# Turning attention rows by TensorE transposes of four blocks instead of a VectorE transpose and four transfers per block

## The chip, the cores and the metric

The kernel runs on one core of a Trainium2 chip. The metric is the device time of one launch in microseconds (us). Before the change it is 474.96 us, the median of 3 runs (473.96 to 475.51). A difference of 0.3% is about what a measurement of this kernel can tell.

## The reference

Two stages follow each other. The first is linear attention with a decay per head (4 batches, 8 heads, 768 positions, head size 64), computed in blocks: each block takes its own masked scores and a running state. The second is a mixture of experts (3072 tokens of 512 features, 8 experts, hidden size 1024, one expert per token).

```
for b in range(nb):                                   # blocks of 64 positions
    intra = (qb @ kb^T * Dmask) @ vb
    inter = (qb * lam_pow) @ kv_state
    out[:, :, sl] = intra + inter
    kv_state = lam_block * kv_state + (kb * rev_pow)^T @ vb
x = out as rows of 512 features, one per token
logits = x @ w_gate + modality_bias[modality_id]
e_idx = argmax(logits);  gate_w = softmax(logits)[e_idx]
for e in range(8):                                    # tokens of expert e
    out[mask] = gate_w[mask] * (relu(x[mask] @ w1[e]) @ w2[e])
```

All is in fp32; the kernel's experts use three products of split fp32 parts per product.

## The kernel before

**Attention.** There are 24 blocks g of 128 tokens (4 batches of 6). A loop over m = 0 to 11 (lines 819 to 888) works on a pair of blocks a = 2m and b = 2m+1. In step m it issues, in this order: `scores` and `mask` of the next pair, `keys` (ScalarE scales the keys, kd, 16 instructions for two blocks) and `query` (GpSimd), then `from_state` and `values` of this pair, whose result `o` in PSUM ScalarE copies to `xt` (line 283), then `products` of the next pair (they need kd), which give the state (`add`, VectorE). Every second step `gates` computes the router's logits of four blocks. Input pairs are fetched into four slots: `load(m + 4)`, 2 MB, is issued on ScalarE's queue in step m (line 88), after the copies of that step.

**The turn.** `o` holds features on partitions; rows to be scattered need tokens on partitions. `turn` (line 287) transposes 32x32 squares of one block on VectorE (`xt` to `xn`), and `spread` (line 301) moves `xn` with four transfers of 64 KB on SP's queue into `grp`, a buffer of 8 token tiles whose rows have 512 features and 16 words of tags. A token tile holds 32 tokens of each of four blocks. 96 such transfers are made.

**Routing.** For each of three groups of 8 token tiles, VectorE chooses experts and slots; GpSimd scatters each tile's rows to the buffer `placed` in HBM (`one_slot`, line 389), which is ordered by expert. `aside` (line 797) says in which step how many of them are issued. Lists of work (`listA`, `listB`, `listC`) are computed for the experts as soon as enough tokens are counted.

**Experts.** A tile of 256 tokens is fetched from `placed` (`fetch_x`, into `xg`), turned on VectorE (`turn_rows`, line 659), and goes through `first_layer` (w1) and `second` (w2); the result `y` is scattered to the output. Tiles 0 to 3 start while the routing still goes on; then come two thin tiles (64 and 32 tokens) and eight more wide ones. Weights are fetched by `fetch_w1` and `fetch_w2`, four transfers each, only if the expert differs from the one before. The scatter leaves the rows behind each expert's last token undefined; `clear_ends` (line 611) writes 256 blank rows there for each of 8 experts, ahead of the fetches of the thin tiles.

**What sets the order.** The orders of TensorE, VectorE, ScalarE and SP are those in which the code is written. Each transfer of SP's and ScalarE's queues signals one of eight counters in turn, and one that is to use a counter again waits until the transfer before it on that counter has landed. A transfer that waits holds up everything behind it on its engine.

Of the kernel before, what the change touches and what calls it, by code (L numbers as in the profile page):

```python
# [15 lines left out]
P = 128  # L16
# [16 lines left out]
RC = B * NC // RN  # L33
GR = B * NC // 4
MIN_WIDE = 8
MAX_WIDE = 17
# [6 lines left out]
def linear_attention_moe(tc, qkv, lam, modality, wg, mbias, w1, w2, out):  # L43
    nc = tc.nc
    with ExitStack() as ctx:
# [105 lines left out]
        def gpsimd_constants():  # L151
            pool(nc.gpsimd.memset(onesb, 1.0))
            pool(nc.gpsimd.affine_select(out=lowb, in_=onesb, pattern=[[1, P]], compare_op=ALU.is_gt,
                                         fill=0.0, base=0, channel_multiplier=-1))
            loose_iota = dict(channel_multiplier=0, allow_small_or_imprecise_dtypes=True)
            pool(nc.gpsimd.iota(desc, pattern=[[-1, E]], base=E, **loose_iota))
            pool(nc.gpsimd.memset(pay, 0))
            for t in range(4):
                mine = pay[t * Q : (t + 1) * Q].rearrange("q (g t) w -> q g t w", t=4)
                pool(nc.gpsimd.iota(mine[:, :, :, 0:1], pattern=[[4 * P, GR], [Q, 4]], base=t * P, channel_multiplier=1))  # L160
# [114 lines left out]
        def values(g):  # L275
            c = g % NC
            vt, op, pt = loaded(g)[2], ops.pop(g), pts.pop(g)
            for p in range(NP):
                for hl in range(2):
                    nc.tensor.matmul(op[place(g, hl), p, :], vt[:, (2 * p + hl) * D : (2 * p + hl + 1) * D],  # L280
                                     pt[:, hl, p, :], start=(c == 0 and p == 0), stop=(p == NP - 1))
            xts[g] = work.tile([P, NP, P], F32, name="xt", bufs=6)
            nc.scalar.copy(out=xts[g], in_=op)  # L283

        xns = {}
# [8 lines left out]
        def group(g):  # L294

            n = B * NC // RN
            if g % n == 0:
                groups.append(work.tile([P, 2 * 4 * RW], F32, name="grp", tag="grp", bufs=RN))
            return groups[g // n].rearrange("p (g c w) -> p g c w", g=2, c=4)[:, g % n // 4]

        def spread(g):

            to = group(g)
            xn = xns.pop(g).rearrange("q t p a -> q t (p a)")
            t = g % 4
            for j in range(4):
                i = j ^ 2 * (g % HB)
                nc.sync.dma_start(out=to[t * Q : (t + 1) * Q, :, i * P : (i + 1) * P], in_=xn[j * Q : (j + 1) * Q])  # L308

        def gates(grp):  # L310
            four = range(4 * grp, 4 * (grp + 1))
            for p in range(NP):
                for t, g in enumerate(four):
                    nc.tensor.matmul(lps[t * Q : (t + 1) * Q, grp % 2, :], wgq[:, g % HB, p, :], xts[g][:, p, :],
                                     start=(p == 0), stop=(p == NP - 1), tile_position=(0, t * Q))
            for g in four:
                xts.pop(g)

# [70 lines left out]
        def one_slot():  # L389
            c, at = slots.pop(0)  # L390
            row = group(c // 4 * 4)[:, c % 4]
            pool(nc.gpsimd.tensor_copy(out=row[:, DM:].bitcast(I32), in_=pay[:, c, :]))
# [213 lines left out]
        def clear(at):  # L606

            nc.sync.dma_start(out=placed[at, :].rearrange("(p r) w -> p r w", p=P),
                              in_=blank.unsqueeze(1).to_broadcast([P, TT // P, RW]))
# [90 lines left out]
        def second(n, t, ticks=(1, 3, 5, 7)):  # L700
# [3 lines left out]
            for f in range(FC):  # L704
# [3 lines left out]
                if f in ticks:  # L708
                    tick(mm)
            y = work.tile([P, DM], F32, name="y", tag="xt", bufs=6)  # L710
            nc.scalar.activation(out=y, in_=yp, func=AF.Copy, scale=idx[:, t, 1:2].bitcast(F32))  # L711
# [32 lines left out]
        def thin_second(n, hnt, w2):  # L744
# [13 lines left out]
            y = work.tile([P, DM], F32, name=f"yn{m}", tag="xt", bufs=6)[:, :w]  # L758
            nc.scalar.activation(out=y, in_=yp, func=AF.Copy, scale=idx[:, 0, 1:2].bitcast(F32))
# [36 lines left out]
        pairs = B * NC // HB  # L796
        aside = {7: (1, 1), 8: (1, 2), 9: (1, 2), 11: (4, 4)}

# [12 lines left out]
        keys(1, True)  # L811
        turn(0)
        add(0)
# [3 lines left out]
        products(1)  # L817
        turn(1)
        for m in range(pairs):
# [15 lines left out]
            if m == 0:  # L835
                keys(2)
                keys(3)
                spread(0)
                spread(1)
            if ahead:  # L840
                for i, g in enumerate((a + 2, b + 2)):
# [4 lines left out]
                    query(g)  # L846
                    if i == 0 and m > 1:
                        spread(a - 1)
            elif m > 0:
                spread(a - 1)  # L850
            do()
# [13 lines left out]
            if m + SLOTS < pairs:  # L865
                load(m + SLOTS)
            if m > 0:
                turn(a)
                spread(a)
# [4 lines left out]
            if m > 0:  # L874
                turn(b)
            go(aside.get(m, (0, 0))[1])
            if m % 2:
                gates(m // 2)
            if m == 6:
# [10 lines left out]
        spread(B * NC - 1)  # L890
        fetch_x(1)
# [183 lines left out]
```

## Time and profile before

| | |
|---|---|
| runs | 475.51, 473.96, 474.96 us |
| profiled execution | 473.02 us, span 471.3 us, clock 0.931 |
| PE busy | 405.5 us (86%) |
| VectorE (DVE) busy | 264.2 us (56%) |
| ScalarE (ACT) busy | 194.7 us (41%) |
| GpSimd (POOL) busy | 99.5 us (21%) |
| attention (step m=2 on) | 34.0 to 129.0 us |
| first tile's first layer starts | 140.6 us |
| thin tiles start on PE | 260.8 us |
| eight wide tiles start | 281.6 us |

The profile is of one execution; its own time is 1.94 us under the median of the runs. A row of the timeline has a start, a length, the engine and line, and in brackets how long the engine was idle before and what ended that. An fp32 matmul shows as two records.

### The profile page before, as it was taken

To read this page: it belongs to the slowest core of one execution; us is meant where nothing else is said; L and a number is where in the kernel's file an instruction comes from. 1 tells how busy PE (TensorE), PEld (TensorE's weight loads), DVE (VectorE), ACT (ScalarE), POOL (GpSimd) and SP (SyncE) were. 2 spreads that over 40 slices of the span, in tenths; PEclk is the share of its full clock that TensorE was granted. 3 is DMA by queue.
4 is the path that set the end of the run, shared out by engine and by line. 5 is a ranking of instruction groups with operands and counts; after the bars stand their busy time and mean duration, and the time that the engine had idled before them with its cause. 6 is when DMAs were issued, how large, how long until landed. Compare 5 with 4: busy or idle time off the path is not lost.

```text
span 471.3 us, 9647 instructions
## 1 busy us (share of the span) xinstructions
PE 405.5 (86%) x3501; PEld 354.6 (75%) x3501; DVE 264.2 (56%) x494; ACT 194.7 (41%) x363; POOL 99.5 (21%) x125
## 2 busy tenths in 40 slices
PE   7688969979809996998619689999999999999991
PEld 4578858868608896896618359898989999898981
DVE  6636546855434774688242137666666665757520
ACT  1514434344302452643141135646464655556420
POOL 3624122552007022820200000202020202020200
PEclk9979888989967997999959999999999999999996
DMA  7979888999946698332533660676730211210100
GB/s 268 392 273 242 271 256 253 345 304 344 247 100 203 217 339 340 137 115 107 212 106 73 225 208 1 174 250 200 272 90 15 78 37 55 45 46 1 46 25 19
DMA packets 52040, 81.67 MB, mean 173 GB/s; under 512 B 8462, under 2 KB 33550, under 8 KB 51728
## 3 DMA queue, kind: packets, MB, share of 16 engines
q1 hardware_dynamic: 43552, 47.22, 33.5%
q10 hardware_dynamic: 4512, 20.97, 13.0%
q0 software_dynamic: 3920, 12.78, 7.2%
q8 instruction: 29, 0.48, 0.4%
q14 instruction: 27, 0.22, 0.2%
HBM read 90.57 MB, written 17.84 MB: 230 GB/s over the span
## 4 chain that ended last, share of the span: by engine, by line
issue 47%; DMA 19%; PE 11%; DVE 8%; POOL 6%; SPq 4%; ACT 2%; POOLq 0%; ACTq 0%; DVEq 0%
DMA grp<-xn 8%; POOL out_dram L712 5%; DMA mod<-in_modality_dram 5%; DMA load<-in_qkv_dram 4%; SPq L308 2%; DMA placed<-blank 2%; PE s L688 2%; ACT kd L228 2%; PE o L668 2%; PE o L669 2%; PE o L670 2%; PE kv L688 1%; DVE pt L242 1%; DVE w2l L580 1%; DVE hl L696 1%
## 5 line engine op out<-in xcount | busy, mean ns | idle before, releaser
L580 DVE TENSOR_TENSOR w2l<-raw,w2h 128x1024 fp32r<-128x1024 f32 x48 | 58.7, 1223 | 48.0 <-ACT w2h L579 48.0
L712 POOL DMA_INDIRECT out_dram<-y,idx x24 | 31.5, 1311 | 229.2 <-ACT y L711 206.2
L668 PE MATMUL o<-w2h,hh 128*128 128x512 f32 x192 | 75.2, 391 | 0.0
L669 PE MATMUL o<-w2l,hh 128*128 128x512 f32 x192 | 75.0, 391 | 0.0
L670 PE MATMUL o<-w2h,hl 128*128 128x512 f32 x192 | 74.9, 390 | 0.0
L668 PE MATMUL kv<-xh,w1h 128*128 128x256 f32 x176 | 52.0, 295 | 13.6 <-DVE hl L696 13.6
L228 ACT ACTIVATE kd<-load,dk 128x64 f32<-128x64 f32 x144 | 35.6, 334 | 51.7 <-DMA grp<-xn 47.9
L579 ACT CAST w2h<-raw 128x1024 fp32r<-128x1024 f32 x48 | 49.8, 1038 | 16.3 <-DMA raw<-in_w_dram 16.3
L580 DVE TENSOR_TENSOR w1l<-raw,w1h 128x1024 fp32r<-128x1024 f32 x44 | 51.3, 1222 | 4.5 <-ACT w1h L579 4.3
L669 PE MATMUL kv<-xl,w1h 128*128 128x256 f32 x176 | 51.5, 292 | 0.0
L670 PE MATMUL kv<-xh,w1l 128*128 128x256 f32 x176 | 51.1, 290 | 0.0
L668 PE MATMUL s<-xh,w1h 128*128 128x256 f32 x176 | 49.9, 283 | 1.2 <-ACT w1h L579 1.2
L670 PE MATMUL s<-xh,w1l 128*128 128x256 f32 x176 | 49.6, 282 | 0.8 <-DVE w1l L580 0.8
L669 PE MATMUL s<-xl,w1h 128*128 128x256 f32 x176 | 49.8, 283 | 0.0
L668 PEld LDWEIGHTS kv<-xh,w1h 128*128 128x128 f32 x176 | 34.9, 198 | 17.6 <-DVE hl L696 13.8
L579 ACT CAST w1h<-raw 128x1024 fp32r<-128x1024 f32 x44 | 43.1, 1045 | 2.5 <-DMA raw<-in_w_dram 2.5
L670 PEld LDWEIGHTS o<-w2h,hl 128*128 128x128 f32 x192 | 36.2, 188 | 7.6
L289 DVE STREAM_TRANSPOSE xn<-xt 128x512 f32<-128x512 f32 x24 | 17.0, 709 | 44.3 <-ACT xt L283 24.7
L669 PEld LDWEIGHTS o<-w2l,hh 128*128 128x128 f32 x192 | 36.2, 188 | 7.2
L668 PEld LDWEIGHTS o<-w2h,hh 128*128 128x128 f32 x192 | 36.2, 188 | 7.2
L250 PE MATMUL kv<-load,kd 128*64 128x64 f32 x320 | 31.1, 259 | 7.9 <-ACT kd L228 7.9
L215 POOL TENSOR_TENSOR qd<-load,pq 128x512 f32<-128x512 f32 x20 | 25.2, 1271 | 58.9 <-DMA load<-in_qkv_dram 41.9
(217 smaller groups left out, 670.2 us busy)
## 6 DMA issues: line engine op xcount, KB each, us to landing
raw<-in_w_dram SPq DMA_DIRECT2D x96, 512.0 KB
load<-in_qkv_dram ACTq DMA_DIRECT2D x8, 2048.0 KB
grp<-xn SPq DMA_DIRECT2D x96, 64.0 KB
xg<-placed SPq DMA_DIRECT2D x48, 128.0 KB
placed<-blank SPq DMA_DIRECT2D x9, 528.0 KB
load<-in_qkv_dram SPq DMA_DIRECT2D x8, 512.0 KB
raw<-in_w_dram ACTq DMA_DIRECT2D x2, 2048.0 KB
both<-in_w_dram SPq DMA_DIRECT2D x8, 512.0 KB
```

The lines of the kernel that those rows point to most:

```text
L215: pool(nc.gpsimd.tensor_tensor(out=qds[g], in0=loaded(g)[1], in1=pq, op=ALU.mult))
L228: nc.scalar.activation(out=kds[g][:, p, hl, :], in_=kn[:, p, hl, :], func=AF.Copy, scale=dk[:, hl, p, P - 1 : P])
L250: nc.tensor.matmul(kp[r, g % HB, p, :], kd[:, p, hl, :], vt[:, (2 * p + hl) * D : (2 * p + hl + 1) * D], start=True, stop=True)
L289: nc.vector.transpose(out=xns[g].rearrange("q t p a -> q p t a"), in_=xts[g].rearrange("q p (t a) -> q p t a", t=4))
L308: nc.sync.dma_start(out=to[t * Q : (t + 1) * Q, :, i * P : (i + 1) * P], in_=xn[j * Q : (j + 1) * Q])
L579: nc.scalar.copy(out=hi, in_=src)
L580: nc.vector.tensor_tensor(out=lo, in0=src, in1=hi.bitcast(F32), op=ALU.subtract)
L668: nc.tensor.matmul(out, ah, bh, start=first, stop=False)
L669: nc.tensor.matmul(out, ah, bl, start=False, stop=False)
L670: return nc.tensor.matmul(out, al, bh, start=False, stop=last)
L688: mm = nc.tensor.matmul(hp[:, j, :], raw1[:, i, kc, fs], xt2[:, kc, :], start=(kc == 0), stop=(kc == KC - 1))
L712: sc = nc.gpsimd.indirect_dma_start(out=out, out_offset=bass.IndirectOffsetOnAxis(ap=idx[:, t, 0:1], axis=0), in_=y, in_offset=None, bound ...
```

## The change

Four blocks' results go into one `xt` tile, in the order 0, 2, 1, 3 of the blocks (the two odd blocks hold their feature halves exchanged). Every second step `turns` makes, for each of the four token tiles of the group, four TensorE transposes into an `o` buffer in PSUM. VectorE copies the upper 64 partitions into the row tile, ScalarE the lower 64 in two copies that undo the exchange. `gates` stands between the second and the third tile. `turn` on VectorE and all 96 `spread` transfers are gone. The order of features in a row is now the natural one, for which w1 is laid out anew on the host.

Beside it: `fetch_x(0)` moves from step 10 to step 9, with `aside` giving step 9 both its scatters early; `clear_ends` moves behind `fetch_w2`, `turn_rows`, `split_rows` and `split_w1` of tile 3, and its eight transfers are declared independent of each other; `y` takes its buffers (4 in place of 6) from another ring.

```
-            xts[g] = work.tile([P, NP, P], F32, name="xt", bufs=6)
-            nc.scalar.copy(out=xts[g], in_=op)
-        def turn(g):
-            xns[g] = work.tile([P, 4, NP, Q], F32, name="xn", bufs=4)
-            nc.vector.transpose(out=xns[g].rearrange("q t p a -> q p t a"),
-                                in_=xts[g].rearrange("q p (t a) -> q p t a", t=4))
+            if g % 4 == 0:
+                xts[g // 4] = work.tile([P, NP, 4, 4, Q], F32, name="xt", bufs=2)
+            nc.scalar.copy(out=xts[g // 4][:, :, :, ORDER.index(g % 4), :], in_=op.rearrange("p a (c t) -> p a c t", c=4))
...
-            for j in range(4):
-                i = j ^ 2 * (g % HB)
-                nc.sync.dma_start(out=to[t * Q : (t + 1) * Q, :, i * P : (i + 1) * P], in_=xn[j * Q : (j + 1) * Q])
+        def turn(grp, tb):
+            tp = ps.tile([P, NP, P], F32, name="o", bufs=2)
+            for p in range(NP):
+                nc.tensor.transpose(out=tp[:, p, :], in_=xts[grp][:, p, tb].rearrange("k t a -> k (t a)"), identity=ident)
+            row = row_tile(4 * grp + tb)[:, :DM].rearrange("t (p h d) -> t p h d", p=NP, h=2)
+            tp = tp.rearrange("t p (h d) -> t p h d", h=2)
+            half = P // 2
+            nc.vector.tensor_copy(out=row[:half], in_=tp[:half])
+            for h in range(2):
+                nc.scalar.copy(out=row[half:, :, h], in_=tp[half:, :, 1 - h])
...
+        def turns(grp):
+            for tb in range(4):
+                if tb == 2:
+                    gates(grp)
+                turn(grp, tb)
+            xts.pop(grp)
...
-                clear(bass.ds(vr, TT))
+                apart("ends", clear(bass.ds(vr, TT)))
...
-        aside = {7: (1, 1), 8: (1, 2), 9: (1, 2), 11: (4, 4)}
+        aside = {7: (1, 2), 8: (1, 2), 9: (2, 0), 11: (4, 4)}
...
             if m % 2:
-                gates(m // 2)
+                turns(m // 2)
...
                 fetch_w2(*fetch_regs(0, True, nc.scalar), eng=nc.scalar)
-            elif m == 10:
                 fetch_x(0)
...
         first_layer(amid2)
-        clear_ends()
         fetch_w2(*fetch_regs(3))
         turn_rows(3)
         split_rows()
         split_w1()
+        clear_ends()
         for n in range(thins, wides + 1):
             fetch_x(n)
```

ScalarE's order in the attention loop, with its waits; DMAHW counters are the eight of the transfers. Before, from the copies of step 2 on (L283; L228 is kd, L88 the load of a pair):

```order
L283 COPY xt<-o 128x512 [waits PE_49] x2
L88 DMA load<-in_qkv_dram 128x4x1024 [waits DMAHW1_49,DMAHW2_49,Activation_49,Pool_49]
L228 ACTIVATE kd<-load,dk 128x64 [waits DMAHW5_49]
L228 ACTIVATE kd<-load,dk 128x64 x7
L228 ACTIVATE kd<-load,dk 128x64 [waits PE_49]
L228 ACTIVATE kd<-load,dk 128x64 x7
L283 COPY xt<-o 128x512 [waits DVE_49,PE_49] x2
L88 DMA load<-in_qkv_dram 128x4x1024 [waits DMAHW3_49,Activation_49,Pool_49]
```

And after the change, the same steps and one group's copies into the rows (L305):

```order
L285 COPY xt<-o 128x16x32 [waits PE_49] x2
L89 DMA load<-in_qkv_dram 128x4x1024 [waits DMAHW2_49,Activation_49,Pool_49]
L229 ACTIVATE kd<-load,dk 128x64 [waits DMAHW5_49]
L229 ACTIVATE kd<-load,dk 128x64 x7
L229 ACTIVATE kd<-load,dk 128x64 [waits PE_49]
L229 ACTIVATE kd<-load,dk 128x64 x7
L285 COPY xt<-o 128x16x32 [waits PE_49] x2
L89 DMA load<-in_qkv_dram 128x4x1024 [waits DMAHW3_49,Activation_49,Pool_49]
L305 COPY grp<-o 64x4x64 [waits DVE_49]
L305 COPY grp<-o 64x4x64
```

Before, a load waits on counters that transfers of `spread` (grp<-xn) took in between; now there are none of those between, and eight copies stand ahead of the next kd every second step.

TensorE's order around step 3. Before (L280 is `values`, L250 `products`, L314 `gates`, L238 `scores`):

```order
L238 MATMUL s<-load 128x128 x16
L272 MATMUL o<-qd,state_120 64x128 x8
L280 MATMUL o<-pt,load 64x128 x16
L250 MATMUL kv<-load,kd 64x64 x16
L314 MATMUL x<-xt,wgq 32x128 x16
L238 MATMUL s<-load 128x128 x16
```

After (L299 are the transposes, L310 `gates`, L239 `scores`):

```order
L239 MATMUL s<-load 128x128 x16
L273 MATMUL o<-qd,state_120 64x128 x8
L281 MATMUL o<-pt,load 64x128 x16
L251 MATMUL kv<-load,kd 64x64 x16
L299 MATMUL o<-ident,xt 128x128 x8
L310 MATMUL x<-xt,wgq 32x128 x16
L299 MATMUL o<-ident,xt 128x128 x8
L239 MATMUL s<-load 128x128 x16
```

Sixteen transposes now stand around the gates, before the next step's scores.

SP's queue at the end of tile 2's first layer. Before (L643 is w1 of tile 3, L608 the clears, L651 w2 of tile 3, behind the eighth clear):

```order
L643 DMA raw_1378<-in_w_dram 128x1024
L614 TENSOR_LOAD ends_at
L614 ISA x2
L608 ISA
L608 DMA placed<-blank 256x1x528
...
L608 DMA placed<-blank 256x1x528
L631 TENSOR_LOAD listB
L631 ISA x2
L634 TENSOR_LOAD listB
L634 ISA x2
L651 ISA
L651 DMA raw_1530<-in_w_dram 128x1024
```

After (L652 is w2 of tile 3, L609 the clears):

```order
L652 ISA
L652 DMA raw_1556<-in_w_dram 128x1024
L615 TENSOR_LOAD ends_at
L615 ISA x2
L609 ISA
L609 DMA placed<-blank 256x1x528
...
L609 DMA placed<-blank 256x1x528
L595 TENSOR_LOAD listC
L595 ISA x2
```

The fetch of w2 moved ahead of the eight clears; the fetches of the thin tiles follow behind them.

## Rows read from the trace of the kernel before

**Rows 1.** Windows: us; PE, PEld, DVE, ACT, POOL busy; PEclk, DMA share, GB/s

```profile
34.00:129.00 95.00, 84.43 (x1299) 72.83 (x1299) 56.22 (x146) 39.80 (x142) 28.81 (x32) 0.93 0.91 280
...
140.00:144.00 4.00, 3.37 (x8) 2.72 (x9) 1.71 (x2) 0.00 (x0) 2.98 (x5) 0.50 0.76 202
...
281.60:471.30 189.70, 179.80 (x1156) 164.16 (x1152) 114.33 (x123) 95.68 (x125) 22.60 (x17) 0.98 0.28 84
```

**Rows 2.** Waits: engine, line, releaser, us in total, times, longest

```profile
ACT kd L228 <- DMA grp<-xn: 47.9, 8, 8.8
...
PE kv L668 <- DVE hl L696: 13.6, 1, 13.6
```

**Rows 3.** Timeline of ScalarE, steps 3 and 4

```profile
45.18 0.38 ACTq L88 DMA_DIRECT2D load<-in_qkv_dram  x1
...
45.60 3.93 ACT L228 ACTIVATE kd<-load,dk 128x64 f32<-128x64 f32 x16 [5.99 <-DMA grp<-xn]
...
49.44 1.04 ACT L283 COPY xt<-o 128x512 f32<-128x512 f32 x2
```

**Rows 4.** Timeline of PE: gates, and scores opening steps 2, 3 and 10

```profile
31.68 1.36 PE L314 MATMUL x<-xt,wgq 128*32 128x128 f32 x32
...
33.98 2.06 PE L238 MATMUL s<-load 64*128 64x128 f32 x32 [0.94 <-DMA load<-in_qkv_dram]
...
39.83 2.06 PE L238 MATMUL s<-load 64*128 64x128 f32 x32
...
116.05 2.06 PE L238 MATMUL s<-load 64*128 64x128 f32 x32
```

**Rows 5.** Timeline from step 11 to the first tile

```profile
123.33 0.43 PE L272 MATMUL o<-qd,state 64*64 64x128 f32 x4 [0.23 <-ACT xt L283]
...
127.92 1.06 PE L314 MATMUL x<-xt,wgq 128*32 128x128 f32 x26 [0.34 <-ACT xt L283]
...
139.27 1.30 DVE L656 STREAM_TRANSPOSE xt<-xg 128x512 f32<-128x512 f32 x2 [6.33 <-DMA xg<-placed]
...
140.63 6.59 PE L688 MATMUL s<-xt,raw 128*128 128x256 f32 x16 [11.65 <-DVE xt L656]
...
147.08 3.70 PE L688 MATMUL kv<-xt,raw 128*128 128x256 f32 x16
```

**Rows 6.** Timeline of SP's queue, tile 3 and thin tiles

```profile
208.32 1.38 SPq L643 DMA_DIRECT2D raw<-in_w_dram  x4
...
210.96 27.63 SPq L608 DMA_DIRECT2D placed<-blank  x8
...
240.43 1.21 SPq L651 DMA_DIRECT2D raw<-in_w_dram  x4
...
242.49 1.94 SPq L597 DMA_DIRECT2D xq<-placed  x4
...
261.72 2.21 SPq L643 DMA_DIRECT2D both<-in_w_dram  x4
```

**Rows 7.** Waits of SP's queue in 203 to 262 us

```profile
SPq L608 <- DMA placed<-blank: 10.7, 6, 1.9
...
SPq L1008 <- DVE nums L334: 6.0, 1, 6.0
```

**Rows 8.** Timeline of PE: thin tile 1's first wait

```profile
266.06 0.59 PE L728 MATMUL s<-both,xf 128*32 128x256 f32 x2 [1.57 <-DMA both<-in_w_dram]
```

**Rows 9.** Timeline of PE: four fp32 transposes of a thin tile

```profile
273.65 0.42 PEld L739 LDWEIGHTS x<-ident,hn 128*128 128x128 f32 x4 [0.41 <-issue]
...
273.65 0.66 PE L739 MATMUL x<-ident,hn 128*128 128x128 f32 x4
```

**Rows 10.** Groups by form: mean ns after busy us

```profile
L289 DVE STREAM_TRANSPOSE xn<-xt 128x512 f32<-128x512 f32 x24 | 17.0, 709 | 44.3 <-ACT xt L283 24.7 <-DMA grp<-xn 13.2 <-ACT w2h L579 5.2
...
L741 DVE COPY hnt<-x 128x512 f32<-128x512 f32 x1 | 0.7, 692 | 10.9 <-PE x L739 10.9
...
L732 ACT ACTIVATE hn<-s 128x256 f32<-128x256 f32 x1 | 0.4, 384 | 8.6 <-PE s L728 8.6
```

More of the change, by code (lines that the diff above doesn't have):

```diff
@@ L34 @@
 GR = B * NC // 4
+ORDER = 0, 2, 1, 3
 MIN_WIDE = 8
@@ L159, in gpsimd_constants @@
                 mine = pay[t * Q : (t + 1) * Q].rearrange("q (g t) w -> q g t w", t=4)
-                pool(nc.gpsimd.iota(mine[:, :, :, 0:1], pattern=[[4 * P, GR], [Q, 4]], base=t * P, channel_multiplier=1))
+                pool(nc.gpsimd.iota(mine[:, :, :, 0:1], pattern=[[4 * P, GR], [Q, 4]], base=ORDER[t] * P, channel_multiplier=1))
             pool(nc.gpsimd.memset(blank, 0.0))
@@ L292, in linear_attention_moe, with row_tile @@
+            nc.scalar.copy(out=xts[g // 4][:, :, :, ORDER.index(g % 4), :], in_=op.rearrange("p a (c t) -> p a c t", c=4))
         groups = []
-        def group(g):
+        def row_tile(c):
             n = B * NC // RN
[L297 to L305, printed above, removed]
-            for j in range(4):
-                i = j ^ 2 * (g % HB)
-                nc.sync.dma_start(out=to[t * Q : (t + 1) * Q, :, i * P : (i + 1) * P], in_=xn[j * Q : (j + 1) * Q])
+            if c % n == 0:
+                groups.append(work.tile([P, n * RW], F32, name="grp", tag="grp", bufs=RN))
+            return groups[c // n].rearrange("p (c w) -> p c w", w=RW)[:, c % n]
@@ L310, in gates @@
         def gates(grp):
-            four = range(4 * grp, 4 * (grp + 1))
             for p in range(NP):
-                for t, g in enumerate(four):
-                    nc.tensor.matmul(lps[t * Q : (t + 1) * Q, grp % 2, :], wgq[:, g % HB, p, :], xts[g][:, p, :],
+                for t in range(4):
+                    nc.tensor.matmul(lps[t * Q : (t + 1) * Q, grp % 2, :], wgq[:, ORDER[t] % HB, p, :], xts[grp][:, p, :, t, :],
                                      start=(p == 0), stop=(p == NP - 1), tile_position=(0, t * Q))
-            for g in four:
-                xts.pop(g)
+        def turns(grp):
[4 more added lines that the diff above has]
+            xts.pop(grp)
@@ L390, in one_slot @@
             c, at = slots.pop(0)
-            row = group(c // 4 * 4)[:, c % 4]
+            row = row_tile(c)
             pool(nc.gpsimd.tensor_copy(out=row[:, DM:].bitcast(I32), in_=pay[:, c, :]))
@@ L606, in clear @@
         def clear(at):
-            nc.sync.dma_start(out=placed[at, :].rearrange("(p r) w -> p r w", p=P),
-                              in_=blank.unsqueeze(1).to_broadcast([P, TT // P, RW]))
+            return nc.sync.dma_start(out=placed[at, :].rearrange("(p r) w -> p r w", p=P),
+                                     in_=blank.unsqueeze(1).to_broadcast([P, TT // P, RW]))
         def clear_ends():
@@ L709, in second @@
                     tick(mm)
-            y = work.tile([P, DM], F32, name="y", tag="xt", bufs=6)
+            y = work.tile([P, DM], F32, name="y", tag="qd", bufs=4)
             nc.scalar.activation(out=y, in_=yp, func=AF.Copy, scale=idx[:, t, 1:2].bitcast(F32))
@@ L757, in thin_second @@
                                      tile_position=(0, j * m))
-            y = work.tile([P, DM], F32, name=f"yn{m}", tag="xt", bufs=6)[:, :w]
+            y = work.tile([P, DM], F32, name=f"yn{m}", tag="qd", bufs=4)[:, :w]
             nc.scalar.activation(out=y, in_=yp, func=AF.Copy, scale=idx[:, 0, 1:2].bitcast(F32))
@@ L811, in linear_attention_moe @@
         keys(1, True)
-        turn(0)
         add(0)
@@ L817, in linear_attention_moe @@
         products(1)
-        turn(1)
         for m in range(pairs):
@@ L837, in linear_attention_moe @@
                 keys(3)
-                spread(0)
-                spread(1)
             if ahead:
@@ L846, in linear_attention_moe @@
                     query(g)
[L847 to L850, printed above, removed]
             do()
@@ L866, in linear_attention_moe @@
                 load(m + SLOTS)
-            if m > 0:
-                turn(a)
-                spread(a)
             if ahead:
@@ L873, in linear_attention_moe @@
                 add(a + 2)
-            if m > 0:
-                turn(b)
             go(aside.get(m, (0, 0))[1])
             if m % 2:
-                gates(m // 2)
+                turns(m // 2)
             if m == 6:
@@ L886, in linear_attention_moe @@
                 fetch_w2(*fetch_regs(0, True, nc.scalar), eng=nc.scalar)
-            elif m == 10:
                 fetch_x(0)
         turn_rows(0)
-        spread(B * NC - 1)
         fetch_x(1)
@@ L1056 @@
         "lam": c(inputs["lam"].reshape(H, 1)),
-        "modality": c(inputs["moe_modality_id"].astype(_np.int64).reshape(GR, 4, 4, Q).transpose(1, 3, 0, 2).reshape(P, B * NC)),
+        "modality": c(inputs["moe_modality_id"].astype(_np.int64).reshape(GR, 4, 4, Q)[:, list(ORDER)].transpose(1, 3, 0, 2).reshape(P, B * NC)),
         "wg": gates,
         "mbias": c(inputs["moe_modality_bias"]),
-        "w1": c(w1.reshape(E, KC, P, 4, 2 * P).transpose(0, 2, 3, 1, 4)),
+        "w1": c(w1.reshape(E, 4, KC, Q, 4, 2 * P).transpose(0, 1, 3, 4, 2, 5).reshape(E, P, 4, KC, 2 * P)),
         "w2": c(inputs["moe_w2"].reshape(E, FC, P, DM).transpose(0, 2, 1, 3)),
```

1 line of the change is left out of this document (removed).

## The prediction

> **What bounds the kernel now.** I read the busy time by windows first, then the waits, and then the timelines around the longest waits. In the windows the reader is to see that the attention loop (34 to 129 us) has no full engine: PE is busy 84 of 95 us, part of that at the pace of what it waits for, VectorE 56, ScalarE 40 [rows 1]. The waits name the cause: ScalarE stood 47.9 us in eight waits ahead of kd until a grp<-xn transfer landed [rows 2]. It is no data that kd needs. On ScalarE's timeline the fetch of a pair is issued at 45.18 us after such a wait, and kd follows at once [rows 3]: the fetch waits for a transfer counter that the turn's transfers had taken, and kd, the products and the state are queued behind it. So the turn, which nobody on this path reads, sets when the next pair is fetched and when kd is made. Step 2, where nothing waits, lasts 39.83 - 33.98 = 5.85 us from scores to scores; from step 2 to step 10 the mean is (116.05 - 33.98) / 8 = 10.26 us [rows 4]. Two more places stand still. Between the last gates (end 128.98) and the first tile (140.63) PE waits 11.65 us for the fetched rows, then runs its first sixteen matmuls in 6.59 us, the next sixteen in 3.70 [rows 5]; the granted clock there is 0.50, the lower of its two levels, 1.2 GHz [rows 1]. And PE stands 13.6 us in tile 3's first layer [rows 2], because the fetch of w2 is issued at 240.43, behind 27.63 us of clears on SP's queue [rows 6].
>
> **The attention loop.** Removed: 24 VectorE transposes at 0.709 us, 17.0 us in all [rows 10], and 96 transfers; with these go the counters that the fetches wait on, so the 47.9 us of ScalarE's waits go. Not all of that is gain, since other things are late next. Added on PE: 96 transposes, 16 per two steps. Four fp32 transposes take 0.42 us of weight loads, 0.66 with the end of the last [rows 9], so 0.105 us each and 1.7 us per two steps. Added on VectorE: 24 copies of half a tile. 512 columns from PSUM took 0.692 us on all partitions; I take the same for 64, 16.6 us in all [rows 10], so VectorE's sum stays. Added on ScalarE: 48 copies of 256 columns at 0.384 us [rows 10], 18.4 us. The copy of `o` writes runs of 32 elements instead of a dense tile; the trace has no such write, so I price it as the copies that there are (1.04 us for two [rows 3]) and give it 0.5 us per pair as the upper bound.
>
> On PE two steps then cost 2 x 5.85 + 1.36 (gates [rows 4]) + 1.7 = 14.8 us, with small gaps 15.1, or 7.55 per step. ScalarE's sum for two steps is 2 x 3.93 (kd) + 2 x 1.04 + 8 x 0.384 + 0.8 (issues) = 13.8 us [rows 3, 10]; VectorE's, from its 56 us per ten steps, about 12, and more in the steps with routing. Three engines near 14 us with a chain between them do not overlap without loss: the second pair of transposes needs the copies of the first to leave its two PSUM buffers, behind gates that hide some of it, and the next kd stands behind eight copies. So I take 8.3 us per step, 10% over PE's own sum. It stays far below 10.26 since the bound of 7.55 is the row nearest in kind: step 2 ran exactly so. The ends are 7.55, and 10.26 if something else holds the same pace.
>
> Step 2 itself starts when its input has landed, 33.98 [rows 4], as now; the first group's transposes and copies at the end of step 1 stand in front of it, so 35. Nine steps at 8.3 end at 109.7. Step 11 has no scores: from its first product to the end of the gates it takes 128.98 - 123.33 = 5.65 us now [rows 5]; with 1.7 us of transposes, and with VectorE's last copy (0.7) and the turned fetch (1.3 [rows 5]) ahead of the first tile, 9.3. The first tile starts at 119.0 in place of 140.63: 21.6 us less. That its rows are there by then rests on `fetch_x(0)` in step 9, whose scatters are of token tiles copied by step 3, and which has SP's queue to itself; if it is late by more than the 9 us after step 10's end, the gap of 11.65 us returns in part. And without a pause ahead of it the first tile starts at the full clock: 6.59 - 3.70 = 2.9 us less.
>
> **One rule against it.** In the trace transposes in fp32 follow each other every 0.105 us [rows 9]. The Trainium skill (TensorE: Matmul & The Clock Gate, Part 4: PE-mode transpose) gives about 275 ns for a 128x128 bf16 transpose within a kernel and 390 ns alone. By that, 96 would cost an estimated 26 us in place of 10, and the sum would come out 16 us later; no run here shows it, and I go by the row, whose transposes are of the same size and type.
>
> **From the first tile to tile 3.** Nothing is changed there but the buffers of y (four instead of six). Each is scattered within one tile's time, so I cost it at nothing, with 2 us either way.
>
> **The clears.** Now SP ends w1's issue at 208.32 + 1.38 = 209.70. The clears' 27.63 us hold 10.7 us of waits for each other and 6.0 us for a VectorE result that the new order asks for later [rows 6, 7], so without them 10.9. In the new order: w2 with its two register loads (1.84 + 1.21 us) to 212.8, the clears from 214.1. Eight times 528 KB at the loop's 280 GB/s [rows 1] need 15 us, so they land at 229.2, and the fetch for the first thin tile, which reads the cleared buffer, starts then. From there to the fetch of the second thin tile's w1 it is 261.72 - 242.49 = 19.2 us of SP's work [rows 6], so 248.4 in place of 261.72: 13.3 us less. PE is ahead of that: without its stall of 13.6 us it reaches thin tile 0 at 247 in place of 260.8, and it is the second thin tile's w1 for which it waits at 266.06 [rows 8]. So 13.3 is taken, not 13.6. The ends are 14.6 (clears not bound by bandwidth) and 6.6 (each clear still takes its (27.63 - 6.0) / 8 = 2.7 us after the other, so they end at 235.7). From 281.6 on PE is busy 180 of 190 us [rows 1] and the change touches nothing there.
>
> **The sum.** 21.6 + 2.9 + 13.3 = 37.8 us off the profiled execution's 473.0: 435.2. The median of the runs is 1.9 us above that execution, so 437.
>
> **The rivals.**
> - *The transfers' bandwidth is the bound of the loop.* For it: DMA share 0.91 in the window. Against: 280 GB/s there include the turn's 6 MB in small pieces, and step 2's pace was reached. Price: from 34 us on some 21.6 MB are to come (seven pairs, two weights, eight scatters); at 280 GB/s this ends at 111, within the forecast; at 240 at 124, and the first tile starts at about 125: 443.
> - *The evictions pace the loop.* ScalarE's copies stand between `o` and the next fetch and kd. For it: three engines near 14 of 15 us. At 9.3 us per step the gain of the loop falls by 9: 446.
> - *The clears become the wait.* They are issued faster but the thin fetches now wait for all eight. At the lower end, 6.6 in place of 13.3: 444.
> - *The change doesn't free the fetches.* They still wait on a counter, now of another transfer. Against: the order shows only counters of early transfers, and none later. Then the loop keeps 10.26, the first tile starts at 136.6, 4.0 us earlier, and 2.9 and 13.3 stay: 455.
> - *Slower: the clock falls in the loop.* Transposes end every second step, and if PE is granted 1.2 GHz for them and what follows, its 75 us for ten steps double: 35 us are lost when this holds for half of the loop, which takes the whole gain; it decides from there, and with the whole loop at this level it is 437 + 75 = 512. For it: PE's clock is 0.93 in the loop and 0.50 after a pause [rows 1]. Against: the pauses that came before it go away. The Trainium skill (the same page and part) says that transposes do not count as work for the clock; no run here shows that yet.
>
> **How the numbers follow.** Forecast 0.52, with its own range of 430 to 443; bandwidth 0.10; evictions 0.17; clears 0.11; fetches not freed 0.05; clock 0.05, of which 0.03 slower than before. A change under 0.3% is what the measurement of this kernel cannot tell; only the clock's middle and a chain of small losses lie there, 0.02. So faster 0.95, same 0.02, slower 0.03. For 8 in 10 the range takes the low end of the step (7.55: 6.8 us less, with the clears' best another 1.3) and the rivals up to 455, or two of the smaller ones together: 425 to 456.
>
> **What would show it.** ScalarE's waits ahead of kd for a transfer gone, and the fetches issued right behind the copies of `o`; scores of step 10 at about 101 in place of 116; four transposes within 0.5 us; first tile at 119, its first sixteen matmuls in 3.7 us at a granted clock of 1.00; no stall in tile 3's first layer; second thin tile's w1 issued some 13 us earlier relative to tile 3. The forecast is wrong if kd waits for the copies, if transposes wait for a PSUM buffer more than 1 us each time, or if the granted clock in the loop is under 0.9.

## The result and the profile after

| | before | after |
|---|---|---|
| median of the runs | 474.46 us (471.87 to 475.51, 4 runs) | 436.97 us (436.37 to 439.30, 4 runs) |
| profiled execution, span, clock | 473.02, 471.3 us, 0.931 | 436.50, 434.8 us, 0.953 |
| first tile starts on PE | 140.63 us | 115.93 us |
| second thin tile's w1 issued | 261.72 us | 222.09 us |
| eight wide tiles start | 281.6 us | 244.8 us |

The ratio is 0.9226, 95% interval 0.9175 to 0.9278: 37.5 us less. The kernel before took 469.98 to 476.45 us (1.4%) in the 40 runs made beside this kernel and those of the experiments, so a difference of two or three us between medians of four to six runs is not settled by the time alone. Slow runs, over 1.5% above the fastest of their kernel, are left out of the medians and ranges given here (one in run 10, two in run 11).

The windows of after: us, length, busy time of PE, PEld, DVE, ACT, POOL, then granted clock, DMA share and GB/s.

```profile
34.00:115.93 81.93, 73.86 (x1374) 64.99 (x1371) 61.70 (x151) 54.41 (x186) 30.23 (x36) 0.98 0.71 260
115.93:207.00 91.07, 85.49 (x493) 76.50 (x494) 64.91 (x164) 41.78 (x56) 28.69 (x34) 0.94 0.64 221
207.00:245.00 38.00, 32.06 (x231) 20.37 (x230) 8.45 (x15) 7.48 (x12) 2.96 (x3) 0.82 0.52 157
245.00:434.80 189.80, 179.63 (x1152) 164.01 (x1152) 114.20 (x123) 95.56 (x125) 22.60 (x17) 0.98 0.28 84
```

The first window runs up to the first tile, that of [rows 1] to the end of the loop on PE; by that end, 113.94 us against 128.98, the loop ends 15.0 us earlier. Its DMA share fell from 0.91 to 0.71, and the wide tiles' 189.8 us are the same as before. The window 207 to 245, the thin tiles, has the lowest clock, 0.82. The waits of ScalarE in the loop (who, releaser, us in all, times, longest):

```profile
ACT grp L305 <- DVE grp L303: 16.0, 11, 5.0
ACT l L335 <- DVE l L335: 5.4, 2, 3.7
ACT xt L285 <- PE o L281: 5.0, 5, 2.5
ACT kd L229 <- ACT grp L305: 0.6, 1, 0.6
```

No transfer is among them; [rows 2] had 47.9 us. The largest is new: ScalarE's copies of a token tile wait for VectorE's copy of the same tile. ScalarE's timeline shows the fetch issued beside the copies of `o`, without a wait, and kd close behind, as against [rows 3]; this is step 2.

```profile
38.52 0.38 ACTq L89 DMA_DIRECT2D load<-in_qkv_dram  x1
38.84 1.07 ACT L285 COPY xt<-o 128x512 f32<-128x512 f32 x2
39.80 3.93 ACT L229 ACTIVATE kd<-load,dk 128x64 f32<-128x64 f32 x16
```

PE's timeline, to be held against [rows 4, 9]: the scores of step 2, the turn of the second group (eight transposes, the gates, eight transposes), one of the fourth, the scores of step 10.

```profile
33.40 2.06 PE L239 MATMUL s<-load 64*128 64x128 f32 x32
...
45.08 1.09 PE L299 MATMUL o<-ident,xt 128*128 128x128 f32 x8
46.10 1.08 PE L310 MATMUL x<-xt,wgq 128*32 128x128 f32 x32
47.40 1.25 PE L299 MATMUL o<-ident,xt 128*128 128x128 f32 x8 [0.22 <-ACT grp L305]
48.59 2.06 PE L239 MATMUL s<-load 64*128 64x128 f32 x32
...
82.53 1.70 PE L299 MATMUL o<-ident,xt 128*128 128x128 f32 x8 [3.57 <-ACT grp L305]
84.16 3.20 PE L239 MATMUL s<-load 64*128 64x128 f32 x32
...
100.96 2.06 PE L239 MATMUL s<-load 64*128 64x128 f32 x32
```

A step takes (100.96 - 33.40) / 8 = 8.44 us, but steps 2 and 3 take only 48.59 - 33.40 = 15.19 us together, 7.60 each. The transposes wait 0.22 us here; the one long wait is in step 7, 3.57 us, where VectorE computes a list of work ahead of its copies. Behind it the granted clock is 0.64 (82.5 to 87.3 us), and the scores take 3.20 us in place of 2.06. Then the first tile, with [rows 5] before:

```profile
114.59 1.29 DVE L657 STREAM_TRANSPOSE xt<-xg 128x512 f32<-128x512 f32 x2
...
115.93 5.41 PE L689 MATMUL s<-xt,raw 128*128 128x256 f32 x16 [1.99 <-DVE xt L657]
...
121.21 3.70 PE L689 MATMUL kv<-xt,raw 128*128 128x256 f32 x16
```

The pause is 1.99 us in place of 11.65. It is VectorE that is late: it turns the rows without waiting for them, right behind its last copies. PE's stall in tile 3's first layer, 13.6 us in [rows 2], is gone; the last figure is the idle time ahead of these matmuls:

```profile
L669 PE MATMUL kv<-xh,w1h 128*128 128x256 f32 x176 | 51.1, 290 | 0.0
```

SP's queue in tile 3, with [rows 6]: the w2 fetch, the clears, the first thin fetch, the second thin tile's w1.

```profile
185.84 1.35 SPq L652 DMA_DIRECT2D raw<-in_w_dram  x4
188.01 11.66 SPq L609 DMA_DIRECT2D placed<-blank  x8
202.43 1.93 SPq L598 DMA_DIRECT2D xq<-placed  x4
...
222.09 1.98 SPq L644 DMA_DIRECT2D both<-in_w_dram  x4
```

And the thin tiles on PE, with [rows 8, 9]:

```profile
219.69 3.67 PE L729 MATMUL s<-raw,xf 128*64 128x256 f32 x32
226.87 2.24 PE L729 MATMUL s<-both,xf 128*32 128x256 f32 x4 [3.50 <-DMA both<-in_w_dram]
...
234.65 1.12 PE L740 MATMUL x<-ident,hn 128*128 128x128 f32 x4
236.54 5.46 PE L756 MATMUL o<-raw,hnt 128*64 128x256 f32 x32 [0.78 <-DVE hnt L742]
```

PE is now early and waits 3.50 us for that w1; the four transposes behind take 1.12 us, where before they took 0.66; the granted clock from 226.8 to 234.7 us is 0.50, the lower of the two levels.

### The profile page after: what moved, and what is told of

Read it like the earlier page. It is cut to its first block, busy times and chain, and to the rows that moved or that the text cites. A ratio compares the mean times of both kernels' runs of the same rounds, so it can differ in the third digit from the quotient of the medians.

```text
span 434.8 us, 9729 instructions
## 1 busy us (share of the span) xinstructions
PE 398.2 (92%) x3597; PEld 347.6 (80%) x3597; DVE 267.1 (61%) x494; ACT 210.5 (48%) x411; POOL 98.7 (23%) x125
## 4 chain that ended last, share of the span: by engine, by line
issue 48%; PE 19%; DVE 11%; DMA 8%; POOL 6%; ACT 4%; POOLq 1%; ACTq 0%; SPq 0%; DVEq 0%
POOL out_dram L713 6%; DMA load<-in_qkv_dram 5%; DMA raw<-in_w_dram 3%; PE o L281 3%; PE o L299 2%; PE s L239 2%; PE s L689 2%; ACT kd L229 2%; PE o L273 2%; PE kv L689 2%; DVE pt L243 2%; DVE state L261 1%; DVE grp L303 1%; ACT xt L285 1%; DVE w2l L581 1%
## 5 line engine op out<-in xcount | busy, mean ns | idle before, releaser
L669 PE MATMUL kv<-xh,w1h 128*128 128x256 f32 x176 | 51.1, 290 | 0.0
L712 ACT ACTIVATE y<-o,idx 128x512 f32<-128x512 f32 x24 | 16.3, 683 | 42.1 <-PE o L671 42.1
L669 PEld LDWEIGHTS s<-xh,w1h 128*128 128x128 f32 x176 | 33.0, 187 | 2.1 <-ACT w1h L580 1.6
```

The costliest lines, as they stand in the source:

```text
L669: nc.tensor.matmul(out, ah, bh, start=first, stop=False)
```

## The experiments

Twelve kernels ran, each beside runs of the kernel before; the medians given are of these runs. The earlier `fetch_x(0)` and the other ring for `y` were not run alone. Single executions differ ahead of the loop: the scores of step 2 start between 32.8 and 37.4 us, so stretches are compared from there on and not by their clock times.

**1. Are the counters the wait? 512-byte transfers put back.**

```
+        spare_rows = dram.tile([B * NC, 4, Q, 4], F32, name="spare_rows")
+        def spread(g):
+            for j in range(4):
+                nc.sync.dma_start(out=spare_rows[g, j], in_=dk[:Q, 0, 0, 0:4])
...
+                    if i == 0 and m > 1:
+                        spread(a - 1)
...
+            if m > 0:
+                spread(a)
```

> The kernel after, with 96 transfers of 512 bytes added on SP's queue, at the places in the order where the turn's transfers stood. They read a constant and write a buffer that nobody reads. Theory (the transfer counters alone made the wait): with 9 transfers to a step and 8 counters, the fetch of a pair again waits for a transfer that itself waited for the fetch before, so fetches land one after the other, some 10 us apart. ScalarE's idle time ahead of kd comes back (40 us and more, ended by a transfer), scores of step 10 at 112 to 117 in place of 101, first tile 12 to 16 us later, 437 + 14 = 451 us (447 to 455). Rival (the turn's data or its VectorE transposes made the wait, by bandwidth or by the chain through VectorE): 48 KB in all cost nothing, ScalarE's idle time ahead of kd stays under 5 us, 437 to 439 us.

Measured: 467.32 us (464.48 to 468.70), 30.4 over after. Scores of step 10 start at 129.33, the first tile at 150.25. 48 KB did this, so the rival falls: the number of transfers alone is enough for such waits. It is more than the kernel before lost, whose scores of step 10 start at 116.05, so the run shows the mechanism and not its size there. The chain of waits of this kernel (start, length, what):

```profile
33.33 10.87 DMA load<-in_qkv_dram
...
53.66 0.42 SPq L291
54.13 1.41 DMA spare_rows<-dk
55.63 9.23 DMA load<-in_qkv_dram
...
68.33 0.46 issue
68.78 2.87 DMA spare_rows<-dk
71.75 0.42 ACTq L89
```

The reader is to see a ring: a fetch lands, then SP can issue the small transfers that waited for its counter (0.42 us each), the last of them lands, and only then the next fetch is issued. In this stretch one fetch is in flight at a time; from 83 us on they are issued 4.5 to 10 us apart. My size was half of the real one: I had not counted that the small transfers' issues stand between two fetches. ScalarE's idle time ahead of kd is 20 us, not 40, and only 13.9 of it end with a transfer; another 11.3 us that do stand ahead of its copies.

**2. The same with 64 KB each** (`512` in place of `4` columns).

> The same, with each of the 96 transfers at its old size, 64 KB, 6.3 MB in all. Theory (counters): as the run with 512 bytes, plus what 6.3 MB more traffic cost a load that is alone in flight, 0 to 4 us: 451 to 455 us. Rival (bandwidth): 6.3 MB at the loop's 260 GB/s are 24 us of the DMA engines over the loop, whose share rises from 0.71 to about 0.95; the loop is then bound by it, and 443 to 450 us result here where the run with 512 bytes stays at 437.

Measured: 465.34 us (462.84 to 466.92). 6.3 MB more move the time by nothing that shows: while the counters hold the fetches, the DMA engines have time left (share 0.78 in 34 to 116 us, 0.61 in run 1). These bytes go to HBM, those of the turn stayed on the chip. Both my sizes were too small, but the comparison with run 1 is what was asked.

**3. The other way: the kernel before with a quarter of the transfers.**

```
-            for j in range(4):
-                i = j ^ 2 * (g % HB)
-                nc.sync.dma_start(out=to[t * Q : (t + 1) * Q, :, i * P : (i + 1) * P], in_=xn[j * Q : (j + 1) * Q])
+            nc.sync.dma_start(out=to[t * Q : (t + 1) * Q, :, :DM], in_=xn.rearrange("q t w -> q (t w)"))
```

> The kernel before, with its VectorE transposes and all bytes of the turn, but one transfer per block in place of four (24 in place of 96). Rows of a token tile land in another order than the reference's; the routing is computed from xt and stays the same. A step then makes 3 transfers in place of 9, and a fetch waits on a counter for one that is 2.7 steps old. Theory (counters): ScalarE's 47.9 us of waits ahead of kd go almost whole, the first tile starts at 115 to 125 in place of 140.6, with no other part of the change: 474 - 22 = 452 us (448 to 459). Rival (the turn's way through VectorE and the transfers is slow in itself, and only TensorE's transposes free the loop): 468 to 474 us.

Measured: 465.74 us (463.52 to 468.12) beside 472.61, ratio 0.9857 (0.9800 to 0.9914): a third of what the theory asked. The edit does more than I said: a row of `grp` now holds pieces of four tokens, so the output is not the reference's, and the pieces moved are 2 KB in place of 512 bytes. No wait for a turn's transfer is left ahead of kd, but others took its place. Its window up to step 10, the waits of ScalarE, of PE and of SP, and the queue that carries the fetches (packets, MB, share of the 16 engines in 34 to 116 us):

```profile
34.00:112.00 78.00, 60.98 (x1091) 54.58 (x1091) 49.44 (x129) 37.14 (x131) 25.97 (x29) 0.89 1.04 293
```

```profile
ACT kd L228 <- DMA load<-in_qkv_dram: 14.6, 4, 5.8
```

```profile
PE s L238 <- DMA load<-in_qkv_dram: 10.7, 5, 4.0
PE s L686 <- DVE xt L654: 6.3, 1, 6.3
```

```profile
SPq L306 <- DMA load<-in_qkv_dram: 21.9, 6, 6.6
```

```profile
q10 hardware_dynamic: 3860, 17.36, 72.6%
```

The same queue in after, then in before, same stretch:

```profile
q10 hardware_dynamic: 3797, 18.11, 59.2%
```

```profile
q10 hardware_dynamic: 3804, 16.45, 59.5%
```

The DMA engines are full (1.04), and both engines wait for the pairs themselves. A MB of fetches takes 82 x 0.726 / 17.36 = 3.43 us of all engines here, 2.68 in after without the turn's transfers, and 2.97 in before with them. Why it takes more is not shown; the share counts the time of packets, and as it reads above 1 it counts some of it twice. Scores of step 10 start at 112.08: of the loop's 15.1 us (116.05 to 100.96) fewer transfers give 4.0, and the next 11.1 need the rest of the turn gone too. That rest is its bytes, VectorE's transposes and the 24 transfers, which still stand 21.9 us behind fetches on SP's queue. The run does not tell them apart; the waits of PE and ScalarE name the loads.

**4. The clears alone, in the kernel before**, moved and declared independent as in the change.

> The kernel before, with the clears alone moved behind tile 3's fetch of w2, turn and splits, and declared independent; the attention is as it was. Theory: this term of the sum stands by itself: 474.3 - 13.3 = 461 us (459.5 to 462.5). Rival (the shift comes only with the earlier loop): 464 us and more.

Measured: 458.06 us (456.70 to 458.72) beside 472.61: 14.5 us less, 1.2 more than expected and outside my limits by 1.4. The term stands without the earlier loop; the rival falls.

**5. The clears back, in the kernel after** (`clear_ends()` ahead of `fetch_w2`, without `apart`).

> The kernel after, with the clears at their old place, ahead of the fetch of w2 for tile 3, and each waiting for the one before: the edit on the clears undone, the rest of the change kept. Theory: PE's stall of about 13 us in tile 3's first layer comes back whole: 437 + 13.3 = 450 us (448 to 453). Rival (the earlier loop gives SP time, so that the old place costs less than before): clears are issued 25 us earlier, but so is everything around them; if VectorE's result that they wait for (6.0 us before) is there sooner, the stall shrinks by up to 6: 444 us.

Measured: 449.52 us (448.69 to 450.89), 12.6 over after. PE's stall is there again (first row below), and the clears take 27.68 us of SP's queue as before, so the rival falls.

```profile
PE kv L669 <- DVE hl L697: 12.1, 1, 12.1
```

**6. The clears in their new place, one after the other.**

```
-                apart("ends", clear(bass.ds(vr, TT)))
+                clear(bass.ds(vr, TT))
```

> The kernel after, with the eight clears in their new place, but each again waiting until the one before has landed (they are no longer declared independent). Theory of the prediction: each takes its 2.7 us after the other, the clears end some 6 to 7 us later, the fetch of the second thin tile's w1 is that much later, and PE waits for it: 437 + 6.7 = 444 us (441 to 446). Rival (the new place alone gives the gain, the waits for each other are hidden): 437 to 439 us.

Measured: 444.82 us (442.97 to 447.45), 7.9 over after. SP's queue, then PE's wait for the first thin tile's w1:

```profile
185.99 25.84 SPq L609 DMA_DIRECT2D placed<-blank  x8
```

```profile
PE s L729 <- DMA raw<-in_w_dram: 9.0, 1, 9.0
```

So of 12.6 us some 4.7 come from the place, 7.9 from the independence. The new wait is the first thin tile's, not the second's as expected.

**7. Each transpose twice.**

```
+                for _ in range(2):
                     nc.tensor.transpose(out=tp[:, p, :], in_=xts[grp][:, p, tb].rearrange("k t a -> k (t a)"), identity=ident)
```

> The kernel after, with each of the 96 transposes made twice (the second overwrites the first with the same values): 96 times some 0.13 us, 12.6 us more on PE. Theory (in the loop of after, PE is the engine with least slack, 74 of 82 us busy): 6 to 12 us more, 443 to 449 us. Rival (copies on VectorE and ScalarE pace the transposes, PE waits for them anyhow): under 3 us more, 437 to 440 us.

Measured: 448.53 us (446.35 to 448.91), 11.6 over after. Sixteen transposes in a row take 1.96 us, eight took 1.09, so 0.11 us each and 96 x 0.11 = 10.6 us added: the whole of it shows in the total. In the profiled execution less shows in the loop itself: from the scores of step 2 to those of step 10 it takes 108.23 - 37.35 = 70.9 us in place of 67.6, 3.3 more for 64 x 0.11 = 7.0 us of transposes, while the wait in step 7 shrinks from 3.57 to 1.52 us and the clock behind it stays up. The rest comes ahead of step 2, where executions differ anyway, and behind step 10 (20.7 us to the first tile in place of 15.0). PE in the loop is nearly full, and at full clock:

```profile
103.43 1.96 PE L300 MATMUL o<-ident,xt 128*128 128x128 f32 x16
```

```profile
34.00:116.00 82.00, 78.45 (x1430) 71.05 (x1430) 61.01 (x148) 52.03 (x180) 29.05 (x34) 1.00 0.72 262
```

One transpose by itself is long beside that spacing; in after, the shortest, the median and the longest in ns:

```profile
L299 PE MATMUL o<-ident,xt x96: 272/273/458, 30.1 to 113.7; 128*128 128x128 f32 x96
```

**8. ScalarE's copies twice.**

```
+            for _ in range(2):
                 for h in range(2):
                     nc.scalar.copy(out=row[half:, :, h], in_=tp[half:, :, 1 - h])
```

> The kernel after, with ScalarE's 48 copies out of PSUM made twice: 48 times 0.33 to 0.38 us, 16 to 18 us more on ScalarE, which stands in the loop at 54 of 82 us. Theory (PE's sum sets the pace, ScalarE has 27 us of slack): 2 to 6 us more, 439 to 443 us. Rival (the evictions pace the loop): nearly all of it shows, 12 to 18 us more, 449 to 455 us.

Measured: 449.48 us (446.31 to 451.69), 12.5 over after. Eight copies take 2.28 us of ScalarE where four took 1.24, so 0.26 us each and 48 x 0.26 = 12.5 us added, and ScalarE is busy 222.6 us in all in place of 210.5. My 16 to 18 us took the length of one copy's record (0.37) as its price; records overlap. So here too the whole of it shows. The rival's size came out. But PE waits for the copies only 6.5 us in the loop (in after 3.8), and ScalarE's sum rises to 57 of 76 us:

```profile
PE o L299 <- ACT grp L306: 6.5, 8, 2.9
```

From step 2 to step 10 the loop takes 110.13 - 37.06 = 73.1 us, 5.5 more for 32 x 0.26 = 8.3 us of copies. Both 7 and 8 cost in full, so a load added to either engine shows. It does not follow that taking it away gains as much, which the next run asks.

**9. ScalarE's copies without the wait for VectorE's.** They touch other partitions of the same tiles.

```
+            upper = nc.vector.tensor_copy(out=row[:half], in_=tp[:half])
             for h in range(2):
-                nc.scalar.copy(out=row[half:, :, h], in_=tp[half:, :, 1 - h])
+                apart(f"half{grp}{tb}{h}", upper)
+                apart(f"half{grp}{tb}{h}", nc.scalar.copy(out=row[half:, :, h], in_=tp[half:, :, 1 - h]))
```

> The kernel after, with ScalarE's two copies of a token tile declared independent of VectorE's copy of the same tile (they read and write other partitions). In after, ScalarE waits for VectorE's copy in the 24 tiles, 16 us in all of the loop, some 2.3 us per group of four, and kd stands behind it. Theory (the copies stand in the chain of the loop, since making them twice cost 12.5 us): 6 groups at 0.7 times 2.3 us, 10 us less, 427 us (425 to 433). Rival (the second engine's copy is hidden behind the gates, and PE's own sum is the pace, since making the transposes twice cost 11.5 us): 435 to 437 us.

Measured: 433.34 us (431.96 to 435.47), ratio 0.9160 (0.9124 to 0.9195), 3.6 under after, with intervals that overlap. The theory's 10 us are not there. The wait is handed on, to PE:

```profile
ACT grp L306 <- PE o L299: 11.4, 11, 2.7
```

From the scores of step 2 (35.48) to those of step 10 (100.20) the loop takes 64.7 us in place of 67.6, and PE is busy 62.33 of the 66.20 us from 34.00 on, at clock 1.00. So the theory that the copies pace the loop falls. PE's own sum is the nearest bound: in after PE is busy 61.70 of the 66.96 us up to step 10. That ScalarE's copies stand close behind it in the chain, so that 12.5 us more show, is argued and not shown, and no run takes work off PE.

**10. The first tile's rows turned before the last copies.**

```
+            if not ahead:
+                turn_rows(0)
             if m % 2:
                 turns(m // 2)
```

> The kernel after, with VectorE's turn of the first tile's fetched rows put ahead of its copies of the last four token tiles, where it idles 3.9 us. Theory: the first tile's matmuls no longer wait 2.0 us for the turn, and without the pause the first sixteen take 3.7 us in place of 5.4: 437 - 3.7 = 433.3 us (432.5 to 435). Rival (the fetched rows land only just before, so VectorE waits and its copies come later): 436 to 438 us.

Measured: 434.90 us (430.29 to 435.90), 2.1 under after, too scattered to tell by time. The profile shows what was meant, the first sixteen matmuls without a wait and at full speed:

```profile
117.48 3.62 PE L689 MATMUL s<-xt,raw 128*128 128x256 f32 x16
```

In that execution the loop began later (step 2 at 36.32 against 33.40), so the second sixteen end at the same time as in after. The pause does not settle the speed, though. The kernel of run 5 has the loop of after, and the same pause of 1.99 us ahead of the first tile, and its first sixteen run at a granted clock of 1.00:

```profile
116.74 3.72 PE L689 MATMUL s<-xt,raw 128*128 128x256 f32 x16 [1.99 <-DVE xt L657]
```

Run 6 gives 3.72 as well, run 11 gives 5.41 like after, all behind 1.99 us. What decides between the two is not shown.

**11. The second thin tile's weights earlier.** `both1` and its `fetch_w1` move right behind `clear_ends()`, `both2` and its `fetch_w2` ahead of `fetch_x(wides + 1)`.

```
         clear_ends()
+        both1 = w1_part("both1", F32, True)
+        fetch_w1(*fetch_regs(thins + 1, True), to=both1)
```

> The kernel after, with the second thin tile's w1 fetched right behind the clears and its w2 ahead of the last wide fetch there. In after, PE waits 3.5 us for this w1, then 1.4 us at the second layer, and the transposes and the second layer run 2.3 us longer at a low granted clock. Theory: 437 - 6 = 431 us (430 to 434). Rival (2 MB more ahead of the thin tiles' rows delay these by 2 MB at 260 GB/s, 7.5 us, and the wait moves to the first thin tile): 436 to 441 us.

Measured: 429.18 us (427.15 to 430.02), ratio 0.9099 (0.9052 to 0.9145), 7.8 under after. No wait for w1, and the transposes and the second layer are back at full speed (in after 1.12 and 5.46 us); the granted clock of 207 to 245 us is 1.00 in place of 0.82. The eight wide tiles start at 235.70 in place of 244.84.

```profile
224.54 1.93 PE L729 MATMUL s<-both,xf 128*32 128x256 f32 x32
226.40 0.66 PE L740 MATMUL x<-ident,hn 128*128 128x128 f32 x4
227.84 3.67 PE L756 MATMUL o<-raw,hnt 128*64 128x256 f32 x32 [0.79 <-DVE hnt L742]
```

**12. The three together (9, 10, 11).**

> The kernel after, with the three edits together: copies independent, first tile's rows turned early, second thin tile's weights fetched early. By the runs one by one these gave about 3, 2 and 7 us, each in a stretch of its own. Theory (they add up): 437 - 12 = 425 us (422 to 428). Rival (the first two share one gain, a first tile that starts without a pause, and only one of them counts): 427 to 430 us.

Measured: 423.54 us (421.73 to 425.90), ratio 0.8960 (0.8923 to 0.8997), 13.4 under after, as the three add up to (3.6, 2.1 and 7.8). This is the fastest version here. Its first tile starts at 115.49 us, 0.4 earlier than in after, and runs its first sixteen matmuls in 3.62 us; the eight wide tiles start at 233.64, 11.2 earlier. The gain of run 9 is not seen in this execution: from step 2 to step 10 its loop takes 101.06 - 32.82 = 68.2 us, after's 67.6. So the time agrees with the sum, but the trace shows the shares of runs 10 and 11 only.

## Why the prediction was right

The forecast was 437, the median is 436.97. By its steps:

- *The wait.* It said that the turn's transfers take the counters that the fetches wait on; that transfers of 512 bytes can do it is shown by run 1. But the step read it as the only limit of the loop. Run 3 shows a second one right behind, with the DMA engines full, at 112 in place of 101 for step 10. The change took both away at once, so the sum did not suffer; a change that had only saved counters would have been forecast at some 452 us, as I did for run 3, and would have come out at 466. The bandwidth rival was right of a kernel that still moves the turn's bytes.
- *Step of the loop.* 8.3 forecast, 8.44 measured. Step 2 starts at 33.40, not 35; steps 10 and 11 with the turn take 115.93 - 100.96 = 15.0 us, not 17.6. So the first tile starts at 115.93, not 119.0: 24.7 us less in place of 21.6. Of the 24.7, 15.1 come up to step 10 and 9.6 behind it, where the earlier `fetch_x(0)` takes part and was not run alone. The 10% over PE's own sum was given to waits of every group for the copies. Those are small, steps 2 and 3 took 7.60 us each; of the 6.8 us that eight steps lie above that, 5.2 are the wait of 3.57 us in step 7 and the slower work behind it (0.5 and 1.1 us), which the prediction did not price. So the size was right in part by luck. That PE is the nearest bound fits runs 7 and 9.
- *Transposes.* 0.105 us each forecast, 0.11 by run 7. The Trainium skill (TensorE: Matmul & The Clock Gate, Part 4: PE-mode transpose) gives about 275 ns for one of 128x128 in bf16 within a kernel; with that as the price of each, run 7 would have cost an estimated 26 us, and it cost 11.6. As the length of one transpose the trace of after agrees, with a median of 273 ns in fp32; but eight of them end 1.09 us after the first began, so they overlap. The prediction set a length against a spacing, and there was no contradiction. The same part of the Trainium skill says that the full clock does not engage for transposes; here, where at most sixteen stand in a row among matmuls (1.97 us), the loop with twice the transposes was granted 1.00, and no run has transposes alone. The same mistake of length for spacing stands in the sum for ScalarE: eight copies at 0.384 us were 3.07 us, and they take 2 x 1.24 = 2.48.
- *Clock at the first tile.* 2.9 us forecast, 6.59 - 5.41 = 1.2 measured. The step's reason failed: there still is a pause, 1.99 us, since VectorE's last copies stand ahead of its turn of the rows, and the first matmuls behind it run at a granted clock of 0.69 (115.93 to 119.63 us). Without the pause they take 3.62 (run 10); with it 5.41 here and 3.72 in runs 5 and 6, so the 1.2 is what this execution gave.
- *From the first tile to tile 3.* Forecast at nothing. w1 of tile 3 is issued at 182.55 in place of 208.32, 25.8 us less; the two terms above give 25.9. Right.
- *The clears.* 13.3 forecast. The second thin tile's w1 is issued 261.72 - 222.09 = 39.6 us earlier, so 13.9 come here; run 4 says 14.5, run 5 says 12.6. The landing of the clears was worked out as 15.1 us after their start; the first thin fetch starts 202.43 - 188.01 = 14.4 after it. Two ends are not worked out from rows: the 14.6 of this term's best case, and the 425 of the range, for which its own sum (6.8 and 1.3 off 437) gives 429.
- *Not in the sum.* From that w1 to the wide tiles it takes 244.8 - 222.1 = 22.7 us, before 281.6 - 261.7 = 19.9: 2.8 us given back. PE is early there now, waits 3.50 us for w1, and its next work runs at a granted clock of 0.50. I had called PE "ahead of that" and priced only the issue, not what the pause does to the clock. Run 11 gets it back and more.

The errors are -3.1, +1.7, -0.6 and +2.8 us, and nearly cancel: 36.5 us off the profiled execution against 37.8 forecast. The 1.9 us added for the median hide most of the rest: after the change the median lies 0.5 us above the profiled execution. The central value was in part luck; the two large terms were right within 3.1 and 0.6 us.

## What to carry to other kernels

A transfer can cost more than its bytes where it shares a ring of counters with others: 96 transfers of 512 bytes cost 30 us in run 1, since a large fetch waited for the transfer eight places before it, and that one for the fetch before. When such a wait is found, ask for the limit right behind it before pricing its removal, here DMA engines that run 3 found full, with 11.1 of the loop's 15.1 us still missing. And where a stall is shortened but not ended, price the work behind it at both levels of the clock: after the pauses of 2.0 and 3.5 us that were left in after, PE's next work took about 1.5 times as long, but after the same 2.0 us in runs 5 and 6 it did not. Last, a record's length is not the price of one more instruction: transposes of 273 ns follow each other every 0.11 us.

## What the runs showed that was not expected

- Transfers of 512 bytes and of 64 KB in the ring cost the same (467.3 and 465.3 us).
- Doubling work on PE (10.6 us) or on ScalarE (12.5 us) costs 11.6 and 12.5 us, but freeing ScalarE of 16 us of waits gives 3.6 at most: a load that shows does not prove that its engine is the bound. Relief of PE was not run.
- Fetches from HBM beside the turn's transfers, which stay on the chip, take 3.43 us of all DMA engines per MB in run 3 and 2.97 in before; in after, without them, 2.68.
- The same pause of 1.99 us ahead of the same sixteen matmuls is followed by a granted clock of 1.00 in some executions (3.72 us) and of 0.69 in others (5.41 us).
